# A transformer layer on one core: how many weight blocks may be under way at once

## The chip, the cores and the metric

The kernel runs on one core of one Trainium2 chip. The metric is device time in microseconds (us) of the whole program; lower is better. A core has a matrix engine (TensorE, PE in the profile), a vector engine (VectorE, DVE), an activation engine (ScalarE, ACT), GpSimd (POOL) and a sync engine (SyncE, SP), which issues DMAs. The engines run in parallel, each through its own list of instructions in a fixed order, and wait for one another through semaphores.

## The reference, cut to what matters

```python
# S = 2048 tokens, D = 1024, H = 32 heads of 32, F = 3584, all bfloat16
h   = x + attention(layernorm(x), wqkv, wo)        # full softmax, no mask
h2  = h + gelu_tanh(layernorm(h) @ w1 + b1) @ w2 + b2
```

Attention computes for each head `softmax(q k^T / sqrt(32)) v`, then multiplies the joined heads by `wo`. No attention output exists before all keys and values of the layer norm are there, so the projections come first; after that, blocks of 256 queries can go through attention, `wo`, the second layer norm and the two feed-forward products one after another.

## The kernel before

The kernel records its work as tasks in a graph (`Graph.add`, L84), one or a few instructions each, with the tiles that each reads and writes. `Graph.schedule` (L109) then plays the tasks through a model of the engines, in which each task has an assumed duration. It fixes, ahead of any run, the order of the instructions on every engine. `Graph.assign` turns dependencies into semaphore waits, and `emit` writes out the instructions. On the chip the order is never changed: an engine whose next instruction waits does nothing else in the meantime. That holds for SP too, which issues all DMAs: a DMA that waits holds back every DMA behind it.

In the plan, a DMA moves `bytes / dma_rate` (280 GB/s), one after another, with a fixed latency on top. Among the DMAs that are ready, SP takes the one with the lowest `prio`, then the one recorded first (L158). There are 24 completion semaphores ("lanes"); a DMA waits for the one before it on its lane (L181 to L186).

The layer in tiles:

- Attention goes in *jobs* of 256 queries and one group of four heads, each of eight *rounds*. A round is eight score matmuls (`qk`, L796), two exponentials of 128x1024 on ACT (L807), eight value matmuls (`pv`, L833) and matmuls with ones for the softmax sums (L862), helped by an addition on DVE (L848). There are 64 jobs, so 512 rounds and 1024 exponentials. In the order on PE each round starts with its `qk`; the planner fills what a round leaves free on PE with other matmuls ("bg": projections, `wo`, feed-forward), all recorded at L556 to L562.
- For a block `u` of 256 queries, `wo(u)` (L932) multiplies by `wo`, loaded as two blocks of 1 MB (`wov`) into the ring of W1. `ln2(u)` (L961) normalizes and sends the result through a DMA transpose (L585) into `hnT`. `ffn1(u)` (L974) multiplies by W1 in 14 blocks of 512 KB, which pass through a ring of four (`a_w1r`). `gelu` (L1005) runs on DVE with one tanh on ACT. `ffn2(u, j)` (L1018) multiplies by half `j` of W2: seven blocks of 512 KB, which pass through a ring of seven (`a_w2r`). It goes over the seven blocks twice, once for each 128 of the 256 tokens (`t`), so a block's place comes free in the second pass and is filled with the block of the next half.
- The order of recording (L1172 to L1187) is `wo(u+1)`, `ffn2(u,0)`, `ln2(u+1)`, `ffn2(u,1)`, `ffn1(u+1)`, each beside the attention of a later block of queries. After the last round come the last `wo`, layer norm and feed-forward blocks alone, with weights in larger rings (`b_w1r`, `b_w2r`) where keys and values had been.
- Loads of W1 blocks, of `wov`, of W2 blocks, of the tiles of x that are added to the attention output (`hch`, 256 KB), and the copies of the normalized x to memory (`x_scratch`, 1 MB) have `prio` 1. Loads of queries (`QT`) and the transposes go ahead of them (-1), stores of the output have 0.

Of the kernel before, what the change touches and what calls it, by code (L numbers as in the profile page):

```python
# [10 lines left out]
E = mybir.EngineType  # L11

P = 128
BF = dt.bfloat16
F32 = dt.float32


class Buf:
# [42 lines left out]
class Graph:  # L61
# [47 lines left out]
    def schedule(self, pick_pe, pool, switch=0.104, dma_rate=280.0, dma_lat=2.1, dma_issue=0.06):  # L109
# [9 lines left out]
        state = {"mode": None, "dma": 0.0}  # L119
        events = []  # L120
        n = 0
        num = {t: i for i, t in enumerate(self.tasks)}

        def release(t):
# [16 lines left out]
        while n < total:  # L141
            if not events:
                raise RuntimeError("schedule: stuck")
            now = heapq.heappop(events)
            while events and events[0] <= now + 1e-9:
                heapq.heappop(events)
            for e in self.ENGS:
                while free[e] <= now + 1e-9:
                    up = upcoming[e]
                    rd = ready[e]  # L150
                    while up and up[0][0] <= now + 1e-9:
                        rd.append(heapq.heappop(up)[2])
                    if not rd:
                        break
                    if e == E.PE:
                        t = pick_pe(rd, now, state, free_banks(now))
                    else:
                        t = min(rd, key=lambda x: (x.prio, num[x]))  # L158
                        if up and t.prio > 0:

                            for (rt, _, u) in up[:6]:
                                if u.prio < t.prio and rt < now + 0.6 * t.occ:
                                    t = None
                                    break
                    if t is None:
                        break
                    rd.remove(t)
                    if t.acq is not None:
                        b = min([x for x in free_banks(now) if x in t.acq.banks], key=lambda x: max([y.done for y in pool[x]], default=0.0))
                        t.deps.update(pool[b])  # L170
                        t.acq.n = b
                        pool[b] = t.acq
                    start = now
                    if e == E.PE:
                        if state["mode"] != t.mode:
                            start += switch
                        state["mode"] = t.mode
                    t.order = len(seqs[e])
                    seqs[e].append(t)
                    if e == E.SP:  # L180
                        k = min(range(self.n_lanes), key=lambda i: lanes[i].done if lanes[i] else 0.0)  # L181
                        if lanes[k] is not None:
                            t.deps.add(lanes[k])
                            start = max(start, lanes[k].done)
                        lanes[k] = t
                        t.lane = k  # L186
                        free[e] = start + dma_issue
                        s0 = max(state["dma"], start + 0.9)
                        state["dma"] = s0 + t.bytes / dma_rate / 1e3
                        t.done = max(state["dma"], s0) + dma_lat - 0.9  # L190
                    else:
                        free[e] = start + t.occ
                        t.done = start + t.occ + t.lat
                    if t.rel is not None:
                        t.rel.rel.append(t)
                        if len(t.rel.rel) == t.rel.nrel:
                            pool[t.rel.n] = t.rel.rel
                        heapq.heappush(events, t.done)
                    heapq.heappush(events, free[e])
                    n += 1  # L200
                    for s in t.succ:
                        s.left -= 1
                        if s.left == 0:
                            release(s)
# [124 lines left out]
def build_kernel(nc, A_x, A_wqkv, A_wo, B_w1, B_b1, B_w2, B_b2, out):  # L329
# [93 lines left out]
    for k in range(6):  # L423
        h, b = sb(k_hi if k == 2 else ph0, "Wall%d" % k, [P, DC, 512], BF, 1, 4)
# [17 lines left out]
    for k in range(2):  # L442
        h, b = sb(xq_lo, "xq%d" % k, [P, DC, 512], BF)
# [60 lines left out]
    w2d = nc.dram_tensor("w2_blocks", [2, FC // 4, P, 4, 512], BF, kind="Internal").ap()  # L504
# [70 lines left out]
    def dma(out_ap, in_ap, nbytes, reads=(), writes=(), prio=0, noncontig=False, after=()):  # L575
        def fn(s):
            if noncontig:
                with nc.allow_non_contiguous_dma(reason="strided gather"):
                    return s.dma_start(out_ap, in_ap)
            return s.dma_start(out_ap, in_ap)  # L580
        return gr.add(E.SP, fn, 0.06, 0.0, reads, writes, prio, nbytes=nbytes, after=after)
# [436 lines left out]
    def ffn2(u, j, wide=False, W=None, banks=None):  # L1018
        R = R2 if wide else R1
        W = W or R1  # L1020
        c = slice(512 * j, 512 * j + 512)
        ws = []
        for q in range(FC // 4):
            s = W.next("w2", W.nw2)
            dma(W.w2[:, s, :, :], w2d[j, q], P * 4096, reads=[B_w2d[j][q]], writes=[W.B_w2[s]], prio=1)
            ws.append(s)
        for t in range(2):
            bank = banks[t] if banks and banks[t] is not None else slot()
# [288 lines left out]
```

## Time and profile before

| what | us |
|---|---|
| three runs | 1079.47, 1082.18, 1081.65; median 1081.65 |
| the profiled execution: its time | 1080.46 |
| the profiled execution: its span, first to last instruction | 1078.7 |
| ACT busy in the span | 1012.8 |
| PE busy in the span | 1041.8 |
| DVE busy in the span | 751.5 |
| first exponential starts | 22.28 |
| last exponential ends | 1012.2 |

Median time from issue to landing, by kind of DMA: W2 blocks 5.6 us (105 loads), W1 blocks 3.7 us (98 loads), `wov` 4.8 us (16 loads of 1 MB), transposes into `hnT` 2.8 us (14).

The profile's busy shares are averages over three stages with different limits: a start of 22 us until the first exponential, 990 us in which exponentials run, and 66 us in which the last token block goes through the feed-forward part. An engine's gap matters in a stage only if that engine is what the stage waits for.

### The profile page before, as it was taken

Reading aid. Unit: us, or ns where it says so; the run is one execution under the profiler, and the core shown is the slowest. Engines: PE = TensorE matmul, PEld = TensorE weight load, DVE = VectorE, ACT = ScalarE, POOL = GpSimd, SP = SyncE. Lnnn points to the kernel's source line nnn. Section 1 sums busy time; section 2 is a strip of 40 time slices with the busy share of each in tenths; the row PEclk is TensorE's granted clock in tenths of the full one; section 3 lists DMA queues with packets and bytes.
Section 4 is the critical chain, followed back from the end, with each engine's and each line's share of the span. In section 5 each row is a group of like instructions: output and inputs, shape, how many; then the busy total and the mean of one; then the engine's idle time right before and its main releaser. Section 6 shows DMA issues by size and latency. Waiting matters only on the chain.

```text
span 1078.7 us, 41723 instructions
## 1 busy us (share of the span) xinstructions
PE 1041.8 (97%) x18987; PEld 608.7 (56%) x19044; DVE 751.5 (70%) x1438; ACT 1012.8 (94%) x1116; POOL 43.4 (4%) x110
## 2 busy tenths in 40 slices
PE   8999999998899999999999999999999999899998
PEld 6566555554344754674475457447545744474483
DVE  8766666566586896698499669849966967596401
ACT  4999999999999999999999999999999999999650
POOL 4200000000010001001000100100010001000100
PEclk9999999999899999999999999999999999899999
DMA  8560544438474645744764574476466455866260
GB/s 233 151 184 21 154 137 119 139 119 296 157 188 134 206 172 181 251 167 154 260 221 168 188 247 165 149 258 221 158 210 233 178 192 206 241 230 238 91 242 20
DMA packets 136177, 196.37 MB, mean 182 GB/s; under 512 B 49216, under 2 KB 100288, under 8 KB 133184
## 3 DMA queue, kind: packets, MB, share of 16 engines
q1 hardware_dynamic: 136000, 193.70, 53.8%
q8 instruction: 149, 2.44, 0.9%
q14 instruction: 28, 0.23, 0.1%
HBM read 177.94 MB, written 27.26 MB: 190 GB/s over the span
## 4 chain that ended last, share of the span: by engine, by line
ACT 74%; PE 24%; DVE 2%; issue 1%; POOL 0%; POOLq 0%
ACT PT L807 67%; PE ps L559 6%; PE ps L562 5%; PE ps L556 5%; ACT uu L1014 4%; PE ps L796 3%; ACT PX L807 3%; PE ps L833 2%; PE ps L862 1%; PE ps L1055 1%; DVE PS L848 0%; PE ps L629 0%; ACT xnT L636 0%; DVE hch L957 0%; DVE st L608 0%
## 5 line engine op out<-in xcount | busy, mean ns | idle before, releaser
L807 ACT ACTIVATE PT<-ps 128x1024 bf16<-128x1024 f32 x992 | 924.5, 1116 | 7.4 <-PE ps L796 7.3
L848 DVE TENSOR_TENSOR PS<-PT 128x1024 bf16<-128x1024 bf16 x431 | 286.8, 686 | 125.8 <-ACT PT L807 65.1
L796 PE MATMUL ps<-QT,KT 32*128 32x256 bf16 x4096 | 205.0, 274 | 8.9 <-ACT PT L807 5.7
L833 PE MATMUL ps<-PT,V 128*32 128x256 bf16 x3968 | 175.7, 274 | 3.6 <-ACT PT L807 3.5
L796 PEld LDWEIGHTS ps<-QT,KT 32*128 32x128 bf16 x4096 | 61.0, 92 | 164.6 <-ACT PT L807 145.3
L862 PE MATMUL ps<-PS,ones 128*32 128x256 bf16 x1756 | 122.2, 274 | 3.0 <-DVE PS L848 2.7
L559 PE MATMUL ps<-hnT,a_w1r 128*128 128x256 bf16 x979 | 119.1, 273 | 1.7 <-DVE hch L1037 0.5
L833 PEld LDWEIGHTS ps<-PT,V 128*32 128x32 bf16 x3968 | 101.6, 97 | 33.4 <-ACT PT L807 6.3
L559 PEld LDWEIGHTS ps<-hnT,a_w1r 128*128 128x128 bf16 x979 | 90.1, 98 | 26.7 <-issue 15.7
L556 PE MATMUL ps<-a_w2r,gT 128*32 128x512 bf16 x1380 | 99.8, 381 | 0.4 <-DVE gT L1016 0.3
L559 PE MATMUL ps<-a_w2r,gT 128*128 128x512 bf16 x390 | 96.2, 380 | 2.8 <-issue 1.9
L556 PE MATMUL ps<-hnT,a_w1r 128*32 128x256 bf16 x2356 | 83.4, 276 | 1.4 <-DVE gT L992 1.0
L992 DVE TENSOR_TENSOR gT<-ps,b1f 128x512 bf16<-128x512 f32 x98 | 67.3, 687 | 14.5 <-PE ps L559 8.0
L1037 DVE SCALAR_TENSOR_TENSOR hch<-ps,hch 128x512 bf16<-128x512 f32 x32 | 22.0, 689 | 72.1 <-PE ps L562 47.1
L556 PEld LDWEIGHTS ps<-hnT,a_w1r 128*32 128x32 bf16 x2356 | 58.5, 97 | 15.2 <-issue 11.7
L559 PEld LDWEIGHTS ps<-a_w2r,gT 128*128 128x128 bf16 x411 | 35.3, 98 | 46.9 <-issue 12.5
L862 PEld LDWEIGHTS ps<-PS,ones 128*32 128x32 bf16 x1756 | 46.3, 96 | 25.1 <-DVE PS L848 8.8
L1014 ACT ACTIVATE uu<-uu 128x1024 bf16<-128x1024 bf16 x49 | 57.2, 1168 | 0.0
L559 PE MATMUL ps<-xnT,Wall 128*128 128x512 bf16 (+1 forms) x256 | 54.0, 344 | 2.4 <-issue 1.0
L556 PEld LDWEIGHTS ps<-a_w2r,gT 128*32 128x32 bf16 x1380 | 29.9, 96 | 25.7 <-issue 15.2
L613 POOL CAST mvb<-mv 128x2 bf16<-128x2 f32 (+1 forms) x25 | 5.1, 211 | 976.4 <-DVE mv L610 976.4
L878 DVE STREAM_TRANSPOSE OD<-ps 128x256 f32<-128x256 f32 x64 | 28.6, 447 | 11.5 <-PE ps L833 5.9
(91 smaller groups left out, 1018.4 us busy)
## 6 DMA issues: line engine op xcount, KB each, us to landing
a_w2r<-w_blocks SPq DMA_DIRECT2D x105, 512.0 KB, 5.6
a_w1r<-w_blocks SPq DMA_DIRECT2D x98, 512.0 KB, 3.7
wov<-wo_blocks SPq DMA_DIRECT2D x16, 1024.0 KB, 4.8
w_blocks<-in_B_w_dram SPq DMA_DIRECT2D x28, 512.0 KB, 4.0
b_w1r<-w_blocks SPq DMA_DIRECT2D x14, 512.0 KB, 4.1
a_w1r<-in_A_wqkv_dram SPq DMA_DIRECT2D x11, 512.0 KB, 5.2
Wall<-in_A_wqkv_dram SPq DMA_DIRECT2D x17, 256.0 KB, 4.5
xrb<-in_A_x_dram SPq DMA_DIRECT2D x16, 256.0 KB, 4.7
```

The lines of the kernel that those rows point to most:

```text
L556: fns.append(lambda p, j=j: p.matmul(psum[32 * j:32 * j + 32, bi(bank), c0:c1], lhsT[:, 32 * j:32 * j + 32], rhs, start=start, stop=stop, ...
L559: t.whole = lambda p: p.matmul(psum[:, bi(bank), c0:c1], lhsT, rhs, start=start, stop=stop, skip_group_check=True)
L562: t = pe(lambda p: p.matmul(psum[:, bi(bank), c0:c1], lhsT, rhs, start=start, stop=stop), occ, reads=reads, writes=[bb(bank)], mode="full" ...
L796: return p.matmul(psum[:, 2 * us[h // 2] + h % 2, 256 * i:256 * i + 256], KT[32 * h:32 * h + 32, g, k0:k0 + P], QT[32 * h:32 * h + 32, qs, :],
L807: act(lambda a, u=u, k=k: a.activation(PTs[s][:, k, :, :], psum[:, 2 * u:2 * u + 2, :], ACT.Exp, bias=0.0, scale=SCALE), 1024, reads=[B_ps ...
L833: fns.append(lambda p, i=i, h=h: p.matmul(psum[32 * h:32 * h + 32, bi(bank), 0:256], V[:, g, 2 * r + i, 32 * h:32 * h + 32], PTs[s][:, h / ...
L848: dve(lambda v: v.tensor_tensor(PS[:, n, :, :], pairs[:, :, 0:256], pairs[:, :, 256:512], ALU.add), c_dve(1024, 2), reads=B_PTs[s], writes ...
L862: fns.append(lambda p, h=h, rhs=rhs, i=i: p.matmul(psum[32 * h:32 * h + 32, bi(bank), 256:512], ones32[:, :], rhs, start=False, stop=last, ...
L878: t = dve(lambda v: v.transpose(OD[:, o, 1, :], psum[:, bi(bank), 256:512]), 0.36, reads=[self.B_O, self.B_D], writes=B_D, prio=-1)
L992: t = dve(lambda v: v.tensor_tensor(g[:, fc:fc + 2, :], psum[:, bi(bank), :].rearrange("p (f c) -> p f c", f=2), b1f[:, fc:fc + 2].unsquee ...
L1014: act(lambda a: a.activation(w, w, ACT.Tanh, bias=0.0, scale=KT2), 1024, reads=[B_uu[i]], writes=[B_uu[i]], prio=-1)
L1037: drop(dve(lambda v, hs=hs, bank=bank, half=half: v.scalar_tensor_tensor(hch[:, hs, c], psum[:, bi(bank), :], half, hch[:, hs, c], ALU.mul ...
```

## The change

A DMA counts as *bulk* if it is at least 512 KB (`UNIT`) and has `prio` 1 or 2. Bulk DMAs are W1 blocks, `wov` and `x_scratch` (`prio` 1) and W2 blocks, whose `prio` goes from 1 to 2. In the plan SP may take a bulk DMA only when, with it, at most three units (`prio` 1) or two units (`prio` 2) are under way, counted over all bulk DMAs in their order of issue; a `wov` block is two units. `behind(t)` finds the DMA that has to be done first. The same DMA is added to the dependencies, so that the program waits for its landing on the chip as well. For bulk DMAs the plan now assumes 350 GB/s in place of 280. The other loads have no such wait, but stand in the same queue.

```diff
+BULK = {1: 3, 2: 2}
+UNIT = 1 << 19
@@ Graph.schedule
+        bulk = []
+
+        def behind(t):
+            k = BULK[t.prio] - t.bytes // UNIT
+            for b in reversed(bulk):
+                k -= b.bytes // UNIT
+                if k < 0:
+                    return b
+            return None
@@
-                        t = min(rd, key=lambda x: (x.prio, num[x]))
+                        go = rd
+                        if e == E.SP:
+                            go = []
+                            for x in rd:
+                                b = behind(x) if x.bytes >= UNIT and x.prio in BULK else None
+                                if b is None or b.done <= now + 1e-9:
+                                    go.append(x)
+                                else:
+                                    heapq.heappush(events, b.done)
+                            if not go:
+                                break
+                        t = min(go, key=lambda x: (x.prio, num[x]))
@@
                     if e == E.SP:
+                        if t.bytes >= UNIT and t.prio in BULK:
+                            b = behind(t)
+                            if b is not None:
+                                t.deps.add(b)
+                            bulk.append(t)
@@
-                        state["dma"] = s0 + t.bytes / dma_rate / 1e3
+                        state["dma"] = s0 + t.bytes / (350.0 if t.bytes >= UNIT and t.prio in BULK else dma_rate) / 1e3
@@ ffn2
-            dma(W.w2[:, s, :, :], w2d[j, q], P * 4096, reads=[B_w2d[j][q]], writes=[W.B_w2[s]], prio=1)
+            dma(W.w2[:, s, :, :], w2d[j, q], P * 4096, reads=[B_w2d[j][q]], writes=[W.B_w2[s]], prio=2)
```

Since the planner decides the order on all engines, the change also moves other instructions. Laid side by side, the two orders are the same on PE for the first 16 rounds, on SP for the first 58 DMAs (108 us into the profiled execution) and on ACT for the first 466 exponentials. The tasks are the same in both, and so is the work on each engine but for its order.

## The prediction

> **What bounds the kernel now.** I read the page first: busy shares, the row of ACT over time, the chain of waits.
>
> ```profile
> span 1078.7 us, 41723 instructions
> PE 1041.8 (97%) x18987; PEld 608.7 (56%) x19044; DVE 751.5 (70%) x1438; ACT 1012.8 (94%) x1116; POOL 43.4 (4%) x110
> ...
> ACT  4999999999999999999999999999999999999650
> ...
> ACT 74%; PE 24%; DVE 2%; issue 1%; POOL 0%; POOLq 0%
> ```
>
> ACT is full from the second slice to the end of the exponentials, and the chain runs over it. So I asked ACT's timeline for its gaps between the first exponential (22.28) and the last (end 1012.2). The bracket is the idle time before a piece and who ended it.
>
> ```profile
> 292.21 8.37 ACT L807 ACTIVATE PT<-ps 128x1024 bf16<-128x1024 f32 x9 [1.55 <-PE ps L796]
> ...
> 303.52 54.58 ACT L807 ACTIVATE PT<-ps 128x1024 bf16<-128x1024 f32 x59 [0.19 <-PE ps L796]
> ...
> 646.20 2.86 ACT L807 ACTIVATE PT<-ps 128x1024 bf16<-128x1024 f32 x3 [0.47 <-PE ps L796]
> ...
> 729.20 8.36 ACT L807 ACTIVATE PT<-ps 128x1024 bf16<-128x1024 f32 x9 [0.22 <-PE ps L796]
> ...
> 917.41 14.83 ACT L807 ACTIVATE PT<-ps 128x1024 bf16<-128x1024 f32 x16 [0.37 <-PE ps L796]
> ...
> 933.74 8.36 ACT L807 ACTIVATE PT<-ps 128x1024 bf16<-128x1024 f32 x9 [1.50 <-PE ps L796]
> ```
>
> That is all: 1.55 + 0.19 + 0.47 + 0.22 + 0.37 + 1.50 = 4.30 us in 990. No gap is put down to a DMA, and the view of all waits names no weight load as the end of a PE wait. The change leaves the 22 us before the first exponential alone. In the 66 us of feed-forward after the last one it spaces out 14 loads of W2, which SP issues from 1020.63 and PE first reads at 1051.65 and 1063.52; at one per 1.8 us (3.6 a pair, below) the seventh lands by 1035 and the last by 1046. **It can therefore win at most 4.3 us, 0.4%; what it can lose has no such bound.**
>
> The two large gaps have one cause, seen in the stretch table around the second (PE, PEld, DVE, ACT and POOL busy, then granted clock, DMA share, GB/s):
>
> ```profile
> 918.00:921.00 3.00, 1.58 (x56) 0.86 (x48) 2.93 (x7) 3.00 (x4) 0.00 (x0) 1.00 0.81 253
> ...
> 924.00:927.00 3.00, 1.77 (x40) 0.60 (x36) 0.97 (x2) 3.00 (x4) 0.00 (x0) 0.96 1.06 391
> ...
> 930.00:933.00 3.00, 3.00 (x60) 1.86 (x52) 0.69 (x1) 2.24 (x3) 0.00 (x0) 0.50 0.30 119
> 933.00:936.00 3.00, 2.44 (x53) 1.37 (x50) 1.38 (x5) 2.26 (x3) 0.00 (x0) 0.91 0.20 68
> ```
>
> From 918 to 930 six rounds have no filler on PE, which is busy 1.6 to 1.9 us of 3. The clock falls to 0.5 at 926.8 (0.96 leaves 0.24 us at half) and is back at 933.5 (0.91, 0.54 us): 6.8 us. The filler that resumes at 930.18, `ffn1(6)`, runs at half speed, and ACT waits. The same happens from 285.0 to 291.8 (granted 0.50 in 285 to 288, 0.86 in 291 to 294), after four rounds without filler.
>
> **The change, part by part.** *The wait of W2.* It bites where the second half of W2 replaces the first, once for each `u` from 0 to 6. SP's and PE's timelines for `u` = 1, and the landing lines of W2 loads alone at 1020, of this pass, and of two W1 loads issued together at 584.35 (minimum, median, maximum):
>
> ```profile
> 509.71 6.13 SPq L580 DMA_DIRECT2D a_w2r<-w_blocks  x7
> ...
> 516.82 0.61 PE L556 MATMUL ps<-a_w2r,gT 128*32 128x512 bf16 x8
> ...
> 526.09 1.24 PE L559 MATMUL ps<-a_w2r,gT 128*128 128x512 bf16 x5 [0.16 <-issue]
> ```
>
> ```profile
> DMA to landing us min/median/max: 3.2/3.2/3.2
> ...
> DMA to landing us min/median/max: 3.8/5.3/6.9
> ...
> DMA to landing us min/median/max: 3.2/3.6/4.0
> ```
>
> Now all seven loads go out in 6.1 us. With two under way, load 3 waits for load 1, 5 for 3, 7 for 5: the seventh lands four landing times after the first issue. Its first matmul is the piece at 526.09 (24 matmuls of 512 columns come before it in the pass: the narrow ones count by fours), 16.4 us after 509.71. So the path is untouched as long as a landing, with SP's reaction, takes at most 16.4 / 4 = 4.1 us. Bounds from the rows: 3.2 alone, 5.3 with up to five under way. I take 3.6, the row with two: 14.4 us, cover 2.0 left, cost 0. If the cover is gone, PE stops inside `ffn2(u,1)`, behind it stands the next `qk`, and ACT idles after the 0.92 us of the exponential it still has. In `u` = 1 the changed order also brings the uses of the first three blocks nearer to their loads: 3.7 to 3.9 rounds from a place coming free to its use, where it was 4.6 to 5.0; at two exponentials, 1.84 us, a round, 7 us. In the unchanged kernel the first issue came 1.7 us after the place came free (508.05, counting PE's matmuls), behind two transposes (1.24 us of issue each), and landed 3.8 later; the third now waits for that. 1.7 + 3.8 + 3.6 = 9.1 us after the first place came free, needed 2.2 (the third place comes free later) + 7.1 = 9.3. Level; I put 0.5, between 0 and 0.8.
>
> [...]
>
> *The waits of W1 and `wov`.* W1's ring of four and its places coming free already space the issues; W1 lands in 3.0 to 4.8 us in `ffn1(2)`, and no four are under way. The second `wov` waits for the first: issues at 668.29 and 673.16 and a longest landing of 5.6 make it at most 0.7 late, and PE turns to it at 680.63, 2.7 after it landed. Cost 0 (0 to 0.7).
>
> *SP's queue.* Behind a waiting block now stand query loads, stores, x tiles and transposes. Query blocks are requested some 57 rounds (105 us) before use, x tiles and stores as far from any reader; the transposes of `u` = 1 are issued at 506.51 and 508.42 and first read at 538.8. Cost 0, as long as they land within 25 us.
>
> *The last block.* The transposes at 911.3 and 916.6 took 8.9 and 8.5 us, eleven blocks being under way; the median is 2.8. That is what the limit shortens. But PE's order decides: `ffn1(6)` stands in the same round (472) in both orders, and the stretch without filler is seven rounds instead of six, since `ffn2(5,1)` is done a round earlier. The second normalization that feeds it moves later, behind DVE's work on round 468. That leaves three rounds and more, 5.5 us, for a transpose: at 2.8, 0; at 8.9, +3.4. I take 0. Of the two clock drops I take the same cost as now: the seventh empty round can bring the fall earlier, so that less filler is hit, or a second one.
>
> *Pauses without a releaser.* At 645.88 and 916.98 PE paused 0.49 and 0.29 us inside a `qk`, for nothing that the profile shows, with DMA traffic dense; ACT lost 0.47 and 0.37 right after. Fewer blocks under way may shorten them: I put -0.4, between 0 and -0.84.
>
> **Sum.** 0.5 + 0 + 0 + 0 - 0.4 = +0.1 on the profiled execution's 1080.46 (span 1078.7 and 1.8 around it). That execution lies 1.2 below the median of 1081.65, and the runs spread over 2.7. I forecast 1081.2, between 1080.6 and 1081.8: **no change**, where 0.3% (3.2 us) is about what a measurement of this kernel can tell.
>
> **Rivals.** *Late W2 (slower).* Loads of two under way land in more than 4.1 us, because transposes, a store and a query load share the same seconds. At 4.5 the seventh is 4 x 4.5 - 16.4 = 1.6 late; less the 0.92 that ACT still has, 0.7, over seven passes +5: 1086. At 5.3 it is 4.8 late, 3.9 net, +27: 1108. For: the median of 5.3, and the transposes in the same place. Against: in that median up to five blocks queue on each other, which the limit removes. It decides from 4.1 us on.
>
> *The gaps close (faster).* The fall of the clock comes early enough to be over before the filler, the pauses go, ACT's gaps vanish: 1081.2 - 4.3 = 1077. For: one more empty round before 930. Against: the fall came 8 us after PE emptied, and with 13.8 us of emptiness a 6.8 us drop starting 8 to 10 us in still reaches `ffn1(6)`. [...]
>
> *It hardly does what it says.* Landings are so quick that a third block seldom waits, and only the plan's order differs: 1081, with W2 issues as dense as now.
>
> **How the numbers follow.** No change 0.50 (0.10 of it the last rival); late W2 or a late transpose 0.30; gaps closed 0.20, of which some stays under 0.3%, as do light cases of late W2. Faster by over 0.3%: 0.19; within: 0.52; slower: 0.29. Its own range of the forecast is 1079 to 1084. The range reaches down to the closed gaps (1077) and up to light lateness in all passes (1088); the heavy case above it I give one in ten.
>
> **What would show it.** Right: W2 issues in pairs, landings near 3.6, no gap of ACT over 1 us but at two clock drops, transposes into `hnT` never over 5 us. Wrong: gaps of ACT at the start of each `ffn2(u,1)`, with `a_w2r` landing over 4.1; or a clock that never falls between 22 and 1012.

## The result, and the profile after

| | kernel before | changed kernel |
|---|---|---|
| runs | 1079.47 to 1082.18, median 1080.82 (6) | 1087.48 to 1092.94, median 1089.53 (6) |
| ratio of the times, 95% interval | 1 | 1.0082 [1.0061, 1.0103] |
| the profiled execution: time, span | 1080.46, 1078.7 | 1088.41, 1086.6 |
| the run of exponentials starts, ends (two single ones stand 5 to 7 us ahead of it) | 22.28, 1012.2 | 21.80, 1019.9 |
| gaps of ACT of 0.15 us and more in this run | 6, together 4.30 | 15, together 9.93 |
| ACT busy in the span | 1012.8 | 1014.8 |

The changed kernel is slower by 0.8%. All of it arises while exponentials run: the last one ends 7.7 us later and the span is 7.9 longer. The work is not quite the same: a filler on PE is either four narrow matmuls or a wide one, and the new order has 28 more narrow fillers, 84 more matmuls in all (19128 weight loads against 19044). The page of the changed kernel, the lines of span, PE, granted clock and the chain of waits (line numbers are 30 higher than before: L826 is the score matmul, L837 the exponential, L586 and L589 the fillers in narrow and wide form, L610 the DMAs, L615 the transposes):

```profile
span 1086.6 us, 41999 instructions
...
PEclk9999999999899999999999999999999999799999
...
ACT 47%; PE 41%; DMA 6%; DVE 4%; issue 1%; POOL 1%; SPq 0%; POOLq 0%; DVEq 0%
...
a_w2r<-w_blocks SPq DMA_DIRECT2D x105, 512.0 KB, 4.3
```

Before, the chain was ACT 74%, PE 24% and no DMA. Now 6% of it is DMA, 4 of these loads of W2, although such a load lands sooner than before (4.3 us against 5.6). The end no longer hangs on ACT alone. ACT's timeline, seven of its fifteen gaps:

```profile
432.36 21.20 ACT L837 ACTIVATE PT<-ps 128x1024 bf16<-128x1024 f32 x23 [0.97 <-PE ps L826]
...
622.38 21.19 ACT L837 ACTIVATE PT<-ps 128x1024 bf16<-128x1024 f32 x23 [0.71 <-PE ps L826]
...
708.08 7.46 ACT L837 ACTIVATE PT<-ps 128x1024 bf16<-128x1024 f32 x8 [0.21 <-PE ps L826]
715.99 23.25 ACT L837 ACTIVATE PT<-ps 128x1024 bf16<-128x1024 f32 x25 [0.45 <-PE ps L826]
...
814.27 21.19 ACT L837 ACTIVATE PT<-ps 128x1024 bf16<-128x1024 f32 x23 [0.70 <-PE ps L826]
...
843.33 1.94 ACT L837 ACTIVATE PT<-ps 128x1024 bf16<-128x1024 f32 x2 [0.53 <-PE ps L826]
...
939.85 3.77 ACT L837 ACTIVATE PT<-ps 128x1024 bf16<-128x1024 f32 x4 [2.56 <-PE ps L826]
```

Each is put down to a score matmul; the question is what held that up. All PE waits between 285 and 1022 us, by what ended them (total, times, longest):

```profile
PE ps L586 <- DMA a_w2r<-w_blocks: 2.7, 4, 0.9
...
PE ps L586 <- DMA hnT<-a_xb: 1.2, 1, 1.2
...
PE ps L589 <- DMA a_w2r<-w_blocks: 0.2, 1, 0.2
```

Neither W2 nor `hnT` stood in this view before. PE's five waits on W2 stand at 431.58 (0.87), 620.84 (0.72), 707.31 (0.20), 715.21 (0.43) and 812.73 (0.71): right ahead of the first five gaps above, and nearly as long (0.97, 0.71, 0.21, 0.45, 0.70). What PE loses there, ACT loses in full. The chain of waits through the first of them, `ffn2(0,1)`:

```profile
415.25 3.69 DMA a_w2r<-w_blocks
418.94 0.02 issue
418.96 3.10 DMA a_w2r<-w_blocks
422.06 0.02 issue
422.08 4.78 DMA a_w2r<-w_blocks
426.86 0.02 issue
426.88 4.66 DMA a_w2r<-w_blocks
431.54 0.04 issue
431.58 0.40 PE ps L586 x4
```

Four landings follow one another, each issue waiting for the landing before: 3.69 + 3.10 + 4.78 + 4.66 = 16.23 us, with 0.06 for SP between them. PE would have gone on at 431.58 - 0.87 = 430.71, 15.5 us after the first issue. In `u` = 2 PE waits for the sixth block, and the order of SP's list adds to the chain. SP's timeline:

```profile
603.24 0.32 SPq L610 DMA_DIRECT2D a_w2r<-w_blocks  x1
603.61 3.23 SPq L615 DMA_TRANSPOSE hnT<-a_xb  x2
606.93 1.02 SPq L610 DMA_DIRECT2D a_w2r<-w_blocks  x2
611.83 0.34 SPq L610 DMA_DIRECT2D out_dram<-hch  x1
612.22 1.47 SPq L610 DMA_DIRECT2D a_w2r<-w_blocks  x2
```

The two transposes stand behind the first block and hold SP, so the second goes out 3.7 us after the first; in the unchanged kernel both transposes stand ahead of the first block, and it is 0.6 us. The fourth block was allowed from 611.20, when the second had landed. But the plan had put an output store ahead of it, and this store waited until 611.83 for a vector instruction. In `u` = 3 and 4 two transposes stand there as well (3.7 and 4.0 us between the first two blocks), and four of the five waits lie in these three passes: three on the sixth block and one, at 707.31, on the second.

The other large gap is that of the last block. Busy time by stretch (PE, PEld, DVE, ACT and POOL, then granted clock, DMA share, GB/s):

```profile
924.00:927.00 3.00, 1.43 (x40) 0.79 (x40) 2.80 (x6) 3.00 (x5) 0.00 (x0) 1.00 0.98 332
927.00:930.00 3.00, 2.67 (x37) 0.77 (x40) 1.61 (x5) 2.96 (x5) 1.81 (x4) 0.52 1.24 197
...
936.00:939.00 3.00, 2.50 (x48) 1.96 (x48) 0.69 (x1) 1.28 (x2) 0.00 (x0) 0.50 0.35 130
939.00:942.00 3.00, 2.60 (x56) 1.23 (x48) 0.79 (x3) 2.15 (x3) 0.00 (x0) 0.71 0.00 0
```

The clock is at 0.5 from 927.1 to 940.8 (0.71 over 3 us leaves 1.74 at half): 13.7 us, twice the 6.8 of before. The two transposes issued in 924 to 931 took 7.5 and 5.4 us; PE waited 1.21 for the second, so the stretch without fillers went on to 936.5, and the clock did not come back in the meantime.

The sum for the profiled execution: gaps +5.6 (9.93 - 4.30), of which W2 3.04, the last block 1.34 (2.56 and 0.28 at 943.90, against 1.50), and pauses of PE without releaser 0.9 (1.96 against 0.47 + 0.22 + 0.37 in ACT's gaps). ACT busy +2.0, because two exponentials after an interruption take 1.94 us and a pair within a run 1.83 to 1.85, and there are more interruptions (26 against 9, short ones counted). Gaps under 0.15 us bring 0.5, the earlier start -0.5. Together 7.6, against 7.7 at the last exponential. That it adds up only says that nothing on ACT's timeline was left out. The waits on W2 are the largest single term, but well under half of the loss.

### The profile page after: what moved, and what is told of

The parts are those of the page before. It is cut to its first block, busy times and chain, and to the rows that moved or that the text cites. A ratio compares the mean times of both kernels' runs of the same rounds, so it can differ in the third digit from the quotient of the medians.

```text
span 1086.6 us, 41999 instructions
## 1 busy us (share of the span) xinstructions
PE 1052.1 (97%) x19128; PEld 608.8 (56%) x19128; DVE 748.8 (69%) x1438; ACT 1014.8 (93%) x1116; POOL 44.4 (4%) x110
## 3 DMA queue, kind: packets, MB, share of 16 engines
q8 instruction: 150, 2.46, 0.9%
## 4 chain that ended last, share of the span: by engine, by line
ACT 47%; PE 41%; DMA 6%; DVE 4%; issue 1%; POOL 1%; SPq 0%; POOLq 0%; DVEq 0%
ACT PT L837 43%; PE ps L589 13%; PE ps L586 11%; PE ps L826 6%; PE ps L592 5%; DMA a_w2r<-w_blocks 4%; PE ps L863 4%; ACT PX L837 3%; PE ps L892 2%; ACT uu L1044 2%; DVE PS L878 1%; DVE hch L987 1%; DVE st L638 1%; DMA hnT<-a_xb 0%; DMA xrb<-in_A_x_dram 0%
## 5 line engine op out<-in xcount | busy, mean ns | idle before, releaser
L837 ACT ACTIVATE PT<-ps 128x1024 bf16<-128x1024 f32 x992 | 923.2, 1085 | 13.4 <-PE ps L826 12.9
L826 PE MATMUL ps<-QT,KT 32*128 32x256 bf16 x4096 | 205.4, 275 | 8.3 <-ACT PT L837 6.7
L826 PEld LDWEIGHTS ps<-QT,KT 32*128 32x128 bf16 x4096 | 61.0, 92 | 163.7 <-ACT PT L837 135.7
L589 PE MATMUL ps<-hnT,a_w1r 128*128 128x256 bf16 x960 | 117.3, 273 | 1.0 <-DVE OD L915 0.6
L586 PE MATMUL ps<-a_w2r,gT 128*32 128x512 bf16 x1420 | 103.2, 381 | 3.4 <-DMA a_w2r<-w_blocks 2.7
L589 PEld LDWEIGHTS ps<-hnT,a_w1r 128*128 128x128 bf16 x960 | 88.0, 98 | 25.9 <-issue 13.6
L589 PE MATMUL ps<-a_w2r,gT 128*128 128x512 bf16 x401 | 98.0, 381 | 0.5 <-DVE hch L1067 0.2
L586 PE MATMUL ps<-hnT,a_w1r 128*32 128x256 bf16 x2432 | 89.1, 277 | 4.3 <-DVE gT L1022 1.2
L586 PEld LDWEIGHTS ps<-hnT,a_w1r 128*32 128x32 bf16 x2432 | 60.5, 97 | 19.8 <-issue 17.6
L589 PE MATMUL ps<-xnT,Wall 128*128 128x512 bf16 (+1 forms) x296 | 63.6, 349 | 0.5 <-ACT xnT L666 0.3
L589 PEld LDWEIGHTS ps<-a_w2r,gT 128*128 128x128 bf16 x401 | 34.4, 98 | 46.9 <-issue 11.8
L1044 ACT ACTIVATE uu<-uu 128x1024 bf16<-128x1024 bf16 x49 | 54.2, 1112 | 0.1
L586 PEld LDWEIGHTS ps<-a_w2r,gT 128*32 128x32 bf16 x1420 | 31.3, 96 | 30.6 <-issue 14.8
L589 PEld LDWEIGHTS ps<-xnT,Wall 128*128 128x128 bf16 x296 | 25.3, 98 | 26.2 <-issue 8.2
```

The source lines that it names most:

```text
L586: fns.append(lambda p, j=j: p.matmul(psum[32 * j:32 * j + 32, bi(bank), c0:c1], lhsT[:, 32 * j:32 * j + 32], rhs, start=start, stop=stop, ...
L589: t.whole = lambda p: p.matmul(psum[:, bi(bank), c0:c1], lhsT, rhs, start=start, stop=stop, skip_group_check=True)
L826: return p.matmul(psum[:, 2 * us[h // 2] + h % 2, 256 * i:256 * i + 256], KT[32 * h:32 * h + 32, g, k0:k0 + P], QT[32 * h:32 * h + 32, qs, :],
L837: act(lambda a, u=u, k=k: a.activation(PTs[s][:, k, :, :], psum[:, 2 * u:2 * u + 2, :], ACT.Exp, bias=0.0, scale=SCALE), 1024, reads=[B_ps ...
L1044: act(lambda a: a.activation(w, w, ACT.Tanh, bias=0.0, scale=KT2), 1024, reads=[B_uu[i]], writes=[B_uu[i]], prio=-1)
```

## The experiments

Each ratio is against the kernel before in the same series (its medians there are 1081.42 to 1083.13, from 16 to 30 runs; in the first series of the changed kernel 1080.82, from 6). It is not the quotient of the two medians and differs from it by up to 0.2% (1.0113 for the changed kernel, again), so rows that lie as near as that are not told apart. The last columns come from one profile each: PE's waits on W2 blocks, and PE's pauses of 0.2 us and more between 285 and 1013 us that no releaser explains, both summed in us.

| kernel | ratio, 95% interval | waits on W2 | pauses |
|---|---|---|---|
| before | 1 | 0 | 1.4 |
| changed | 1.0082 [1.0061, 1.0103] | 2.9 | 2.0 |
| changed, again | 1.0093 [1.0068, 1.0117] | 6.3 | 0.7 |
| changed, shifted by 96 instructions | 1.0099 [1.0071, 1.0128] | 4.5 | 2.7 |
| changed order, no waits | 1.0048 [1.0028, 1.0069] | 1.9 | 1.1 |
| old order, waits | 1.0077 [1.0051, 1.0104] | 4.8 | 6.5 |
| changed order, waits of W2 alone | 1.0117 [1.0090, 1.0143] | 6.9 | 3.7 |
| changed order, waits of W1 and `wov` alone | 1.0048 [1.0031, 1.0065] | 3.4 | 0.3 |
| three units for W2 | 1.0020 [1.0003, 1.0037] | 0.2 | 0.9 |
| rank and rate | 1.0034 [1.0016, 1.0052] | 1.9 | 2.9 |
| rate alone | 1.0036 [1.0017, 1.0054] | 1.3 | 2.6 |
| second half of W2 free | 1.0066 [1.0037, 1.0095] | 0 | 5.6 |
| second half of W2 free, shifted by 96 | 1.0028 [1.0008, 1.0048] | 0 | 4.4 |
| limit with the old rate | 1.0022 [1.0006, 1.0038] | 2.6 | 1.5 |
| three units for W2, old rate | 1.0010 [0.9997, 1.0024] | 0.3 | 2.0 |
| before, busy PE | 1.0013 [0.9996, 1.0029] | 0 | 3.9 |
| before, shifted by 32 | 0.9991 [0.9973, 1.0009] | 0 | 1.0 |
| before, shifted by 96 | 0.9978 [0.9961, 0.9994] | 0 | 2.1 |
| before, shifted by 160 | 1.0004 [0.9988, 1.0019] | 0 | 1.6 |
| before, busy PE, shifted | 0.9998 [0.9981, 1.0016] | 0 | 3.6 |

### Waits or order

The theory was that the waits on the chip make W2 late; the rivals, that the new order does, or that the last block carries the loss (the "two windows" below are its drop of 13.7 us, 927.1 to 940.8, twice the 6.8 of before). Four kernels separate order and waits.

```diff
 # changed kernel, plan untouched
-                            if b is not None:
-                                t.deps.add(b)
```

> The changed order of instructions on all engines, but none of the added waits is put into the program (the plan is the same, SP issues a bulk load as soon as its place is free). Theory 'late W2' (the chain of four landings on the chip makes the second half of ffn2 late): the gaps of ACT put down to W2 loads, 0.97 + 0.71 + 0.21 + 0.45 + 0.70 = 3.0 us in the changed kernel, go, and with them about one more us of shorter ones; 1085 to 1086.5, against 1089.5 with the waits. Theory 'order' (where the planner now puts the fillers on PE costs the time, and the waits are covered): 1088.5 to 1090.5, with the gaps still there. Theory 'last block' (the double clock drop at 927 to 941 is most of the loss): the drop stays two windows long, with the transposes later still, because more blocks are under way; 1088 or more.

```diff
 # kernel before, in Graph.schedule, after the plan has chosen t; W2 loads marked with kind = "w2"
+                        if t.bytes >= UNIT and t.prio == 1:
+                            room = (2 if t.kind == "w2" else 3) - t.bytes // UNIT
+                            for x in reversed(bulk):
+                                room -= x.bytes // UNIT
+                                if room < 0:
+                                    t.deps.add(x)
+                                    break
+                            bulk.append(t)
```

> The unchanged kernel's order of instructions on all engines, with the added waits alone: a W2 load waits until with it at most two units are under way, W1, wov and the copies of x at most three. Theory 'late W2': the unchanged order issues seven W2 loads back to back and now spaces them like the changed one, and its fillers use them as soon; 3 to 5 us over the unchanged kernel, 1084 to 1086. Theory 'order': the waits are covered, 1080 to 1082. Theory 'last block': at 911 to 926 fewer blocks are under way when the transposes go out, they land sooner, and the single clock drop stays; 1080 to 1081.

```diff
-                            if b is not None:
+                            if b is not None and t.prio == 2:
```

> The changed order with the waits of W2 blocks alone; W1, wov and the copies of x wait for nothing but their places. Theory 'late W2': all of the loss is there, 1088.5 to 1090.5, and four landings in a chain as before. If the waits of W1 and wov carry a part of it (a W2 load also waits behind a waiting W1 load in SP's queue), 1086 to 1088.

```diff
-                            if b is not None:
+                            if b is not None and t.prio == 1:
```

> The changed order with the waits of W1, wov and the copies of x alone; W2 blocks wait for nothing but their places. Theory 'late W2': as without any added wait, 1085 to 1086.5. If the waits of W1 and wov carry a part, 1087 or more.

Measured: order alone 1.0048, waits alone 1.0077, waits of W2 alone 1.0117, waits of W1 and `wov` alone 1.0048. So "late W2" and "order" are both true in part: either half of the change loses time by itself, and the two do not simply add up. The waits of W1 and `wov` cost nothing on top of the order. The waits alone lose 8 us, where I had expected 3 to 5; in the profile of that kernel the pauses (6.5 us, below) are longer than the waits on W2 (4.8), so not all of this loss is late W2. Waits on W2 are there in all four kernels, also in the one without any added wait. Its SP timeline in `ffn2(4,1)`, and PE's wait behind it (line numbers are 2 lower than in the changed kernel):

```profile
801.56 0.34 SPq L608 DMA_DIRECT2D out_dram<-hch  x1
801.94 0.93 SPq L608 DMA_DIRECT2D a_w2r<-w_blocks  x2
805.65 0.32 SPq L608 DMA_DIRECT2D QT<-q_scratch  x1
806.01 1.77 SPq L608 DMA_DIRECT2D a_w2r<-w_blocks  x2
```

```profile
810.48 1.05 PE L584 MATMUL ps<-a_w2r,gT 128*32 128x512 bf16 x16 [0.74 <-DMA a_w2r<-w_blocks]
```

Here the W2 blocks wait for no landing; they stand in SP's list behind a store and a query load that wait for DVE and PE. The plan held the blocks back, took these small DMAs in the meantime, and the list on the chip keeps that order.

### Which part of the rule

```diff
-BULK = {1: 3, 2: 2}
+BULK = {1: 3, 2: 3}
```

> As the changed kernel, but three units may be under way for W2 too, so a block waits for the third before it and the seventh block of a half lands three landings after the first issue instead of four. Theory 'chain of landings': at 4.3 us (the median of W2 landings in the changed kernel) to 5 us each that is 13 to 15 us, inside the 16.4 of cover; the gaps of ACT put down to W2 go or halve, 1.002 to 1.005 of the time before (1.008 with two). If the limit as such is not the cause, 1.007 or more.

```diff
-                                b = behind(x) if x.bytes >= UNIT and x.prio in BULK else None
+                                b = None
@@
-                            if b is not None:
-                                t.deps.add(b)
```

> Only the rank (W2 behind W1 and wov) and the assumed 350 GB/s are left of the change; the plan has no limit and the program no wait. Theory 'limit in the plan': the changed order lost 1.0048 without any wait on the chip because the plan held W2 blocks back and so put them behind stores and query loads in SP's list; without the limit SP issues the seven back to back as before, and the time is 0.998 to 1.002 of the time before. Theory 'rank': W2 behind W1 is enough to make it late, 1.003 to 1.006.

```diff
-            dma(W.w2[:, s, :, :], w2d[j, q], P * 4096, reads=[B_w2d[j][q]], writes=[W.B_w2[s]], prio=2)
+            dma(W.w2[:, s, :, :], w2d[j, q], P * 4096, reads=[B_w2d[j][q]], writes=[W.B_w2[s]], prio=2 if j == 0 else 1.5)
```

> As the changed kernel, but the W2 blocks of the second half (ffn2(u,1)) stand outside the rule: they do not wait and are not counted, and rank between W1 and the W2 blocks of the first half. W1, wov, the copies of x and the first half keep their limits. Theory 'the second half replaces the first': the loss is gone, 0.999 to 1.003 of the time before, no PE wait on a W2 block. If it is the limit on the other loads or the rest of the plan, 1.005 or more.

Then, to divide rank and rate, the kernel with rank and rate once more with `prio=1` for W2:

> The plan assumes 350 GB/s for bulk loads; W2 keeps the rank of W1, no limit, no waits. If the rank made W2 late in the run with rank and rate (1.0034, PE waits of 1.31 and 0.57 us on W2 blocks): no wait on W2, 0.999 to 1.002. If the rate did: 1.003 to 1.005, with waits on W2.

and the whole change, with two and with three units for W2, at the old rate:

```diff
-                        state["dma"] = s0 + t.bytes / (350.0 if t.bytes >= UNIT and t.prio in BULK else dma_rate) / 1e3
+                        state["dma"] = s0 + t.bytes / dma_rate / 1e3
```

> The changed kernel with the plan's 280 GB/s for all DMAs; limit, rank and waits as in the change. Theory 'two under way is the cause': waits of PE on W2 blocks as before the edit, 1.006 to 1.010. Theory 'the plan expects landings too early': at 280 GB/s a block takes 1.87 us of the plan instead of 1.50, the plan brings the uses later, and the loss falls to 1.001 to 1.004.

> As the run before, with three units for W2 as well. With three under way and 350 GB/s the time was 1.0020 of the time before. If rate and limit add up: 0.998 to 1.001. If three under way costs by itself: 1.001 to 1.004.

Three units took all but 0.2 us of the waits on W2 away, as the chain of landings says, and left 1.0020, although a block then lands in 5.2 us (median) instead of 4.3. Rank and rate without any limit, 1.0034, was not the "as before" that I expected; the rate alone gives the same, 1.0036, so it is the rate and not the rank. Without the limit the rank changes nothing at all: the two kernels have the same order on every engine, so their two rows also show how far one order varies from profile to profile. SP's and PE's timelines of the kernel with the rate alone, in `ffn2(2,1)`:

```profile
602.66 0.32 SPq L608 DMA_DIRECT2D a_w2r<-w_blocks  x1
603.02 4.50 SPq L613 DMA_TRANSPOSE hnT<-a_xb  x2
607.57 3.76 SPq L608 DMA_DIRECT2D a_w2r<-w_blocks  x6
```

```profile
613.12 1.05 PE L584 MATMUL ps<-a_w2r,gT 128*32 128x512 bf16 x16 [1.28 <-DMA a_w2r<-w_blocks]
```

One block goes out, then two transposes hold SP for 4.5 us, then the other six. In the unchanged kernel both transposes are issued before the first block (601.17 and 603.09, first block 604.38). PE waits for the second block, issued 4.9 us after the first and landed at 613.08. One way in which the rate makes blocks late can be read from SP's lists of all kernels. Where the plan has 350 GB/s for the blocks of the second half, the two transposes stand behind the first block in `u` = 2, 3 and 4, and the second goes out 3.6 to 5.0 us after the first; where it has 280 GB/s for them, none stands there in these passes, and it is 0.4 to 1.3 us.

The old rate with limit, rank and waits all in place is the strongest of these results: 1.0022, against 1.0082 to 1.0099 in three series of the changed kernel. With three units as well it is 1.0010, and no loss can be told. So the limit, planned at the old rate, does not cost 0.8%, and neither does the rate alone (1.0036); together they do. Whether they do more than add up (that would be 1.0058) the intervals leave open. A limit that the plan does not know of costs without the new rate too: the old order was planned at 280 GB/s, and with the waits put in it lost 1.0077. The code says how limit and rate can combine. In the plan a block that nobody is ahead of lands 0.9 + 512 KB / rate + 1.2 us after its issue: 3.60 us at 350 GB/s, 3.97 at 280. On the chip the median in `ffn2(0,1)` is 4.2 (3.1 to 4.8). In a chain of four, the plan is 2.4 us too early with the one and 0.9 with the other. This is worked out from the code, and the two runs fit it; the new rate also puts the transposes behind the first block, and no run separates the one from the other. Not all waits on W2 go with the old rate: three remain, 2.6 us, in the wide form (972, 980, 1003), and ACT's gaps around them are 0.2 us.

Freeing the second half of W2 did what the theory says to the waits (none left), and not to the time: 1.0066, where I had expected 0.999 to 1.003. With `prio` 1.5 these blocks also stand outside `BULK` and have 280 GB/s in the plan again, so the run takes limit and rate from them at once. PE's waits in that profile instead:

```profile
PE ps L586 <- issue: 3.8, 6, 1.3
...
PE ps L826 <- issue: 1.2, 2, 0.9
```

"issue" is time for which the profile has no releaser. That needed a series of its own.

### Pauses without a releaser, and the clock

The kernel with the old order and the waits has the most of them. One, on PE at 653.32 (L872 is the matmul with ones there):

```profile
651.37 0.29 PE L872 MATMUL ps<-PS,ones 128*32 128x256 bf16 x3
653.32 0.39 PE L872 MATMUL ps<-PS,ones 128*32 128x256 bf16 x5 [1.66 <-issue]
```

PE stops in the middle of a group of eight like matmuls. The view of DMA queues (packets, MB, share) has two queues named "instruction". From 645 to 650.7 queue q8 moves nothing and stands in no line; from 650.7 to 651.8 it moves one packet:

```profile
q1 hardware_dynamic: 655, 1.77, 89.2%
q14 instruction: 1, 0.01, 0.3%
```

```profile
q1 hardware_dynamic: 46, 0.03, 9.5%
q8 instruction: 1, 0.02, 5.6%
```

The packet is 16384 bytes and ends at 651.75; PE goes on 1.57 us later. It is so at every pause over 0.4 us in this kernel: packet ends at 459.96, 477.09, 748.80, 977.00, PE resumes at 461.33, 478.37, 750.14, 978.43, each 1.28 to 1.43 later. The kernel before has 149 such packets for 38,088 matmuls and weight loads of PE (twice its 19,044 weight loads), the changed kernel 150 for 38,256: one for 255 to 256. In the twenty profiles 79 of the 81 pauses of 0.2 us and more end 1.2 to 1.6 us after the end of a packet, while packets are 6.8 us apart on average. To see whether the place of the blocks matters, the kernel before was shifted in PE's list without any change of order:

```diff
+        half = [lambda p, c=c: p.matmul(psum[:, 6, c:c + 128], ident[:, :], b2t[:, c:c + 128], start=True, stop=True) for c in (0, 128)]
-        pe(lambda p: p.matmul(psum[:, 6, 0:256], ident[:, :], b2t[:, 0:256], start=True, stop=True), 0.18 if k < 42 else 0.115,
+        pe(half if k < 16 else lambda p: p.matmul(psum[:, 6, 0:256], ident[:, :], b2t[:, 0:256], start=True, stop=True), 0.18 if k < 42 else 0.115,
```

> The unchanged kernel with the same order and work; 16 of the 80 warm-up matmuls of the first 15 us are split into two of half the width, which moves everything behind them by 32 instructions in PE's list. Instruction blocks are loaded 256 at a time, so their borders then fall elsewhere in the dense feed-forward stretches. Theory 'instruction blocks': the pauses without releaser (before: 646, 729, 917) change place and size, and with them the time, anywhere from 0.999 to 1.005 of the time before. Theory 'DMA traffic alone': they stay where they are, and the time is 0.999 to 1.001.

> As the run with 32, with 48 of the warm-up matmuls split: 96 instructions. Theory 'instruction blocks': pauses at other places again, 0.999 to 1.005. Theory 'DMA traffic alone': 0.999 to 1.001, pauses at 646, 729 and 917.

> As the run with 32, with all 80 warm-up matmuls split: 160 instructions. Theory 'instruction blocks': pauses at other places again, 0.999 to 1.005. Theory 'DMA traffic alone': 0.999 to 1.001, pauses at 646, 729 and 917.

The pauses moved: 646, 729 and 917 in the kernel before; 459 and 948 shifted by 32; 728, 741 and 825 by 96; 537, 549, 741 and 855 by 160. The times moved little, 0.9978 to 1.0004; the lowest lies outside what I had expected. The changed kernel was run again and shifted too, and so was the one with the second half free:

> The changed kernel itself, a second profile and its time against the kernel before in the same series as the next three. Theory 'late W2': the gaps of ACT at the second halves (around 432, 622, 708 to 716, 814, 1010) come again at the same places with 0.2 to 1 us each, since order and waits are fixed. Pauses of PE that no releaser explains (458, 555, 745, 843, 976 in the first profile): if they come from late instruction blocks, they come again within a few us of the same places, because the same 256 instructions are loaded there. Ratio 1.006 to 1.010.

> The changed kernel, its order and waits, shifted by 96 instructions. Theory 'late W2': the waits on W2 blocks are the same, 1.006 to 1.011, with gaps of ACT around 432, 624, 712 to 720, 816 and 1010 to 1018. If the loss hangs on where the instruction blocks begin: 1.000 to 1.004.

> The run with the second half of W2 outside the rule, its order and waits, with 48 split warm-up matmuls, so that every block of 256 instructions begins 96 instructions earlier in the work. If its loss of 1.0066 sits in late instruction blocks (5.7 us of pauses in its profile), it changes: 1.000 to 1.004, with pauses elsewhere. If it sits in the order of the tasks, it stays at 1.005 to 1.009.

That pauses moved under a shift does not show by itself that block borders carry them, since they also move without one: the changed kernel, again, has them at 459, 749 and 765, where the first profile had 456, 554, 745, 842 and 975. Two of five places came again, not all as I had expected. The ends of the packets are the better evidence.

The loss of the changed kernel does not hang on the blocks: 1.0093 and 1.0099, with PE's waits on W2 again in `ffn2(0,1)`, `ffn2(2,1)` and `ffn2(3,1)`, and now also in `ffn2(6,1)`. Their size varies; of the three profiles of this order the second has the most. Its two longest gaps, behind waits of PE on W2 of 1.10 and 1.04 us (at the second the clock also fell to 0.5, from 1014.9 to 1018.3):

```profile
435.78 4.70 ACT L837 ACTIVATE PT<-ps 128x1024 bf16<-128x1024 f32 x5 [2.00 <-PE ps L826]
...
1017.77 4.69 ACT L837 ACTIVATE PT<-ps 128x1024 bf16<-128x1024 f32 x5 [2.51 <-PE ps L826]
```

The second half free went from 1.0066 to 1.0028 with the shift. The intervals still touch (1.0037 and 1.0048), and both lie above 1. The two profiled executions took 1088.08 and 1088.18, with 5.6 and 4.4 us of pauses, so the profiles do not show the difference. Part of that loss can be late instruction blocks, the rest is in the order, and how much is which stays open.

Last, what the clock drops are worth: in the kernel before, groups of matmuls with a zero tile ahead of value matmuls in the two stretches without fillers.

```diff
+    fill = {143: 4, 144: 8, 145: 8, 467: 6, 468: 5, 469: 6, 470: 7, 471: 7, 472: 7}
+    for t in gr.seqs[E.PE]:
+        nr += t.kind == "qk"
+        if nr in fill and t in spare_pv:
+            t.fns = spare_pv[t] * fill.pop(nr) + t.fns
```

> The unchanged kernel, its order and its waits, with matmuls with a zero tile put in front of value matmuls in the two stretches without fillers (20 sets of four before 285 us, 32 sets between 918 and 930); they add zero to the sums and keep PE busy. It measures what the two clock drops cost: if the clock falls for want of work on PE, the granted clock stays at 1.00 in both places, the gaps of 1.55 and 1.50 us go, and the time is 0.996 to 0.998 of the time before. If the drops come from something else, they stay, 0.999 to 1.002; over 1.002 if the added matmuls delay the scores.

> The unchanged order with the zero matmuls of the run with a busy PE (208 more instructions from 293 us on) and 72 split warm-up matmuls (144 more from the start), 352 in all, which is 96 more than a whole block of 256; the shift by 96 alone ran 0.9978. If the busy PE was worth 2 to 3 us and the shifted block borders gave it back: 0.994 to 0.998. If the borders carry nothing: 1.000 to 1.002, as with the busy PE alone.

The stretch table with busy PE, around the second drop, and ACT's gap behind it (L809 is the exponential there):

```profile
918.00:924.00 6.00, 4.56 (x128) 2.65 (x120) 4.54 (x10) 6.00 (x8) 0.00 (x0) 1.00 1.11 304
924.00:930.00 6.00, 5.17 (x152) 3.28 (x144) 2.08 (x3) 6.00 (x7) 0.00 (x0) 1.00 1.12 287
930.00:936.00 6.00, 4.60 (x136) 3.24 (x136) 1.39 (x2) 4.69 (x6) 0.00 (x0) 1.00 0.43 139
```

```profile
933.32 10.23 ACT L809 ACTIVATE PT<-ps 128x1024 bf16<-128x1024 f32 x11 [1.31 <-PE ps L798]
```

With PE busy 76 to 86% the clock holds at 1.00 through the second stretch. The drops from 285 and from 927 are gone, and the gap at 292 shrinks from 1.55 to 0.28. But the time is 1.0013, and 0.9998 shifted: nothing won. (Matmuls and weight loads come one to one, 19128 of each in the changed kernel, so the 208 are 416 instructions and the shifted kernel has 560 more than the kernel before, 48 over two whole blocks. It does not have the borders of the shift by 96 that it was meant to have.) The gap at 934 stays almost as long, since a late instruction block (packet until 931.61, PE on at 933.00) has taken the place of the slow clock. A drop of 3.4 us now stands at 265, with gaps of 0.37 and 0.53 behind it, as it does in the kernels shifted by 32 and by 96, which have no zero matmuls, and there are pauses at 743 and 970 (0.79 and 0.86 us on PE). No kernel of these beats the kernel before by more than 0.3%; the best, its own order shifted by 96 instructions, has 0.9978 [0.9961, 0.9994].

## Why the prediction was wrong

I forecast 1081.2 and no change; the median is 1089.53, above the range's end of 1088.0. By its steps:

- *ACT bounds, at most 4.3 us to win, no bound on the loss.* Right. The loss came as gaps of ACT.
- *The wait of W2, cost 0.* This is the step that failed, in five places. First the landing: "I take 3.6, the row with two". That row was of two W1 loads with nothing else under way. Among stores and transposes the chain of four in `ffn2(0,1)` took 16.29 us (431.54 - 415.25), 4.07 a landing with SP's reaction. That is still just under the 4.1 from which I had said that it decides. Second the cover: I took 16.4 us from `u` = 1 for all passes. `u` = 1 is a pass with no gap in this profile; its seventh block landed 526.35 - 509.98 = 16.4 us after the first issue, exactly at the cover. In `u` = 0 the cover was 15.5, and PE waited 0.87. Third the start of the chain: in `u` = 2, 3 and 4 the second block went out not 0.6 but 3.7 to 4.0 us after the first, and PE waited for the sixth block, which three landings after the second was late; I had sums for the seventh block and, in `u` = 1, the third. Fourth the discount of 0.92 us "that ACT still has": PE's waits of 0.87, 0.72, 0.20, 0.43 and 0.71 cost ACT 0.97, 0.71, 0.21, 0.45 and 0.70. In these stretches PE has no lead left. Fifth, I listed the 350 GB/s in the change and gave it no price. With the old rate and everything else in place the loss is 1.0022. The 0.5 that I put on the third block of `u` = 1 came to nothing in the first profile and to 0.60 us of PE's time in the second.
- *The waits of W1 and `wov`, cost 0.* Right: with them alone 1.0048, with no wait at all 1.0048.
- *SP's queue, cost 0.* I looked at what stands behind a waiting W2 block, and in these passes nothing there was late. What was late are W2 blocks behind other DMAs: two transposes behind the first block in `u` = 2, 3 and 4, the store at 611.83, and in the kernel without waits the query load at 805.65. The order of SP's list was known ahead of the run; I asked it the wrong question.
- *The last block, 0.* Mis-sized: +1.34 in the first profile, through transposes of 7.5 and 5.4 us where I took 2.8, and a clock drop of 13.7 us, twice 6.8, which I had named as possible. In the other two profiles of this order the gap there is 1.51 and 1.54, as before the change: this term lies between 0 and 1.3.
- *Pauses without a releaser, -0.4.* Wrong in sign in this profile (ACT lost 1.96 instead of 1.06), but the three profiles of the changed order have 0.7 to 2.7 us on PE against 1.4, so the term is not settled either way. What the pauses go with is the end of an instruction packet, 1.2 to 1.6 us before PE goes on in 79 of 81 pauses, which I had not looked for.
- *Rivals.* "Late W2" had the right mechanism and place, and a chance of 0.30. Its point of decision, 4.1, was too high and its price, +5 at a landing of 4.5, too small, because of the same cover and the same discount. "The gaps close" did not happen; the busy PE took the drops away and won nothing that can be measured. "Hardly does what it says" did not happen: the blocks go out one behind another.
- *What would show it wrong* was named rightly, but for the place within the pass: gaps of ACT at `ffn2(u,1)` came in four of the seven passes, all but one late in the pass, with a median W2 landing of 4.3.

## What to carry to other kernels

The limit on loads under way turned a stream into a chain of landings. With k of n blocks allowed, the last arrives about n/k landings after the first issue (here all seven had landed 12.6 to 14.6 us after the first issue before, 1.8 to 2.1 us a block, and 16.3 to 18.8 after), and this has to be set against the shortest cover of all passes, not against one. A planner's assumed time for a load must then be its landing time with everything else in the queue, since a chain multiplies the error. And in a list of fixed order, what the plan holds back ends up behind whatever it took in the meantime; so for each moved load ask what it now stands behind, as well as what stands behind it.

## What the runs showed of the hardware

The view of queues has the packets of q8, named "instruction", on the same 16 DMA engines as the data (0.9% of their span in the kernel before, the data's queue 53.8%). They are of 16384 bytes, one for 255.6 matmuls and weight loads of PE in the kernel before and for 255.0 in the changed kernel. In the fifteen profiles that hold a record of every matmul I set the start of each packet between 285 and 1013 us against the moment at which PE had begun 256 k + 150 instructions, k being the packet's number (the 150 is only a common zero). With no DMA of SP under way a packet started 1.58 us after that on average (201 packets), with one 2.09 (487), with three 2.64 (294), with five 3.80 (48); in the first profile of the changed kernel it was 1.53 with none (12), 1.98 with one (28) and 2.46 with three (18). The number of DMAs was not varied by itself, so this is a correlation. Where PE ran the narrow form of the feed-forward it executed 62 a microsecond (315 between the packets at 453.77 and 458.84 of the kernel with the old order and the waits), so that 256 lasted 4.1 us there. The longest pause after a packet's end was 1.81 us (until 973.39 in the shifted changed kernel; packet until 971.91). Most packets had no pause behind them: from 285 to 1013 us the kernel before has 107 packets and 3 pauses of 0.2 us and more, the changed kernel 107 and 5, and the pauses of a run come to 0.3 to 6.5 us.

The granted clock's drops in the twenty profiles lasted 3.41, 6.83, 10.24 or 13.65 us, but for the one that the end of a run cuts short: 6.83 from 285.0 and from 926.7 in the kernel before, 6.83 from 285.4 and 13.65 from 927.1 in the changed kernel. With PE busy 76 to 86% (4.56, 5.17 and 4.60 of 6 us between 918 and 936, before with busy PE) the clock stayed at 1.00; after a stretch with 48% (1.43 of 3 us, 924 to 927 in the changed kernel) it fell. How soon it fell was not the same: in the kernel before the last filler ends at 917.9, PE is busy 1.58 of 3 us from 918 to 921 at a clock of 1.00, and the drop begins at 926.7, 8.8 us after the filler; in the changed kernel the last filler ends at 921.6 and the drop begins at 927.1, 5.5 us later.
